# Packed attention and a feed-forward layer on one core: another order of loads, conversions and batch 1's steps in the start of the kernel

## The chip, the cores and the metric

The kernel runs on one core of one Trainium2 chip. The metric is the device time of one execution in microseconds, the median of three runs. Beside the runs there is one profiled execution, from which every row below comes.

## What is computed

For each of 8 batches and 8 heads, 32 packed queries p attend over 576 keys and values; then the 576 queries q attend over the 32 packed results, which serve as keys and as values. The outcome goes through a feed-forward layer with a leaky activation that has its own slope for each of 2048 columns. Inputs are float32 and the output is float32.

```python
def sm_attn(qq, kk, vv):
    s = scale * np.matmul(qq, kk.transpose(0, 1, 3, 2))
    s = s - np.max(s, axis=-1, keepdims=True)
    a = np.exp(s)
    a = a / (np.sum(a, axis=-1, keepdims=True) + 1e-09)
    return np.matmul(a, vv)
p_packed = sm_attn(p, k, v)
out = sm_attn(q, p_packed, p_packed)          # (8, 8, 576, 64)

h = x @ w_in                                  # x: 4608 x 512, w_in: 512 x 2048
g = np.maximum(h, 0.0) + alpha * np.minimum(h, 0.0)
return (g @ w_out).astype(np.float32)         # w_out: 2048 x 512
```

The two weights reach the kernel as 64-bit words (float64) and are made into float32 on the chip.

## The kernel before

**Tiles and stages.** The packed results of a batch are multiplied into w_in first (packed_w, which gives pw), so that the first product of the feed-forward layer takes the softmax of q directly: a step first(k, f) multiplies pw of 128 columns f into the softmax of one half batch k (288 tokens), and ScalarE (L787) and VectorE (L801) make the activation of it; second(k, f) multiplies the activation into piece f of w_out. order lists all pairs (k, f): for k 0 and 1 f 0 to 3, then f 4 to 7, then k 2 and 3 with f 0 to 7, then k 0 to 3 with f 8 to 15, then the other batches in turn. The main loop (i) runs first two steps ahead of second. The first eight steps are plain float32 (L774 and L896); later ones split each number into two parts (L780 to L782, L899 to L901). In the trace a float32 matmul leaves two records.

**Pieces of the weights.** w_in has eight pieces n (two for each group j of 512 columns) and w_out eight pieces g of 256 rows. Each is loaded by one 1 MB transfer (w_in_load, w_out_load) into a raw tile of const; the tags (wo0 to wo7) are shared, so w_in 0, 3 and 4 use one buffer in turn (wo4), w_out 0 and 1 that of batch 0's k, w_out 2 and 3 that of batch 0's v. A piece is converted in one of two ways. to_f32 (a whole piece): the magnitude of the upper words, a conversion of the lower words on ScalarE, then four passes of VectorE (L132, L135, L139, L143). to_half: the magnitude, a sign and a conversion of the lower words on ScalarE (L175, L176), then three passes of VectorE (L166, L169, L177), at half the value. The magnitude is an Abs on ScalarE (L151) or, for w_in 0 alone, a bit mask on VectorE (L123). w_in groups 2 and 3 and all of w_out but piece 2 are halves. Converted w_in goes to DRAM also (w_whole), for the later batches.

**The order.** attention(b) is a generator; each next() traces one part of it up to its yield. For batches 0 and 1 the parts are: 1 loads packed p and k, 2 loads v, 3 loads q, 4 makes the scores of p on k, 5 and 6 the exponentials, 7 and 8 transpose them, 9 multiplies with v, 10 transposes the result (p2), 11 and 12 make the scores of q, 13 to 15 do the softmax of the first half of the tokens (m, the maxima; z, the sums; then the transposition into a_f, L568), 16 to 18 that of the second half. go(what) reads a string: a and b trace the next part of batch 0 and 1, i and o load the next piece of w_in and w_out, I and O convert it, 0 makes a piece of pw for batch 0, H splits a half of batch 0's softmax, S splits one of the first two pieces of w_out, u, v, w and x put spare matmuls on TensorE (keep_busy; v behind m, w behind z). One string stands ahead of the loop, and pieces holds one for some of its steps. turns and joints place the parts of the later batches, PAIRS the pieces of pw for batches 0 and 1.

The instructions of an engine are put into its queue by the tile framework's planner: by the order in which they are traced and by when its costs say that their inputs are there, so a later one may overtake one that is not ready. issue_after forbids that for the pairs it names: in the start string every load is chained to the one traced before it (load, queue), and a conversion stands behind the last ScalarE and VectorE instruction of batch 0 so far (tail). In the loop the pieces stand behind the activation of the step (marks).

Of the kernel before, what the change touches and what calls it, by code (L numbers as in the profile page):

```python
# [27 lines left out]
def pack_attention_ffn_kernel(  # L28
# [90 lines left out]
    def to_f32(raw, mag, on_dve=False):  # L119
        u, up, low = words(raw, "low", U32)  # L120
        bits = mag.bitcast(U32)
        if on_dve:
            nc.vector.tensor_scalar(  # L123
                out=bits, in0=u[:, :, :, 1], scalar1=0x7FFFFFFF, scalar2=None, op0=ALU.bitwise_and
            )
        else:
            magnitude(mag, up)
        with ExitStack() as behind:
            for mark in late + lows:
                behind.enter_context(tc.issue_after(mark.ins))  # L130
            lows[:] = [nc.scalar.activation(out=low, in_=u[:, :, :, 0], func=AF.Copy, scale=2.0**-29)]
        nc.vector.tensor_scalar(  # L132
            out=mag, in0=mag, scalar1=F64_BOTTOM, scalar2=F64_TOP, op0=ALU.max, op1=ALU.min
        )
        nc.vector.tensor_scalar(  # L135
            out=bits, in0=bits, scalar1=3, scalar2=0x3FFFFFF8,
            op0=ALU.logical_shift_left, op1=ALU.bitwise_and,
        )
        nc.vector.scalar_tensor_tensor(  # L139
            out=bits, in0=u[:, :, :, 1], scalar=0xC0000000, in1=bits,  # L140
            op0=ALU.bitwise_and, op1=ALU.bitwise_or,
        )
        last = nc.vector.tensor_tensor(out=bits, in0=bits, in1=low, op=ALU.add)  # L143
        if len(first_half) == 1:
            first_half.append(last)

    def magnitude(mag, up):
# [5 lines left out]
    def to_half(raw, mag, begun=False):  # L153
# [10 lines left out]
        if not begun:  # L164
            magnitude(mag, up)
# [27 lines left out]
    first_half, begun = [], []  # L193
    last_mm, queue, written, raws, tail, whole, w0, other = [], [], [True], {}, {}, [], [], []

    def half(g):
        return g != 2

    def half_in(j):
        return j > 1  # L200
# [5 lines left out]
    def w_out_convert(g):  # L206
# [8 lines left out]
        if half(g):  # L215
            to_half(raws.pop(("o", g)), mag, g in begun)
        else:
            to_f32(raws.pop(("o", g)), mag)
        if g >= QF:
            w_out_split(g, mag)  # L220

    def w_out_begin(g):
        whole.append(const.tile([P, QF, 2, 512], F32, name="wo_whole", tag="wo7"))
        raw = raws["o", g]
        up = raw.bitcast(F32).rearrange("p a (f t) -> p a f t", t=2)[:, :, :, 1]
        nc.scalar.activation(out=whole[0][:, g], in_=up, func=AF.Abs)
        begun.append(g)
# [29 lines left out]
    def w_in_convert(n):  # L257
# [3 lines left out]
        if half_in(j):  # L261
            to_half(raw, w)
        else:
            to_f32(raw, w, n < 1)
# [686 lines left out]
    counts = dict.fromkeys("iIoOSH01A", 0)  # L951
# [3 lines left out]
    def go(what):  # L955


        for ch in what:
# [9 lines left out]
            elif ch in counts:  # L968
# [9 lines left out]
                else:  # L978
                    with ExitStack() as behind:
                        for ins in tail.values() if ch != "A" else []:  # L980
# [3 lines left out]
                            "O": w_out_convert, "S": w_out_late_split, "H": late_a, "A": w_out_begin,  # L984
# [5 lines left out]
    go("inaaauoiaaaIaboaiiaa0abooavbawaOIx")  # L990
# [16 lines left out]
    PAIRS = {13: ((1, 0), (1, 1)), 31: ((0, 2), (1, 2)), 35: ((0, 3), (1, 3))}  # L1007
# [13 lines left out]
    pieces = {0: "aab", 1: "Oai0ib", 3: "bbI", 4: "I", 5: "Oob0", 6: "bbbiO", 7: "HHbb", 10: "S", 11: "S", 12: "b", 13: "bb", 14: "b", 15: "o", 17: "Io", 18: "b", 19: "I", 20: "i", 21: "o", 22: "I", 24: "I", 27: "O", 30: "O", 34: "O", 36: "O"}  # L1021

    X = {1: 50, **{b: begins[b] + 8 for b in range(2, 7)}}
    Y = {1: 54, **{b: begins[b] + 22 for b in range(2, 7)}}
    for b in range(2, B):
        T, x, y = begins[b - 1], X[b - 1], Y[b - 1]
        if b == 2:
            firsts = [39, 40, 41, 42, 44, 45, 46, 47, 49]
        elif b == 3:
            firsts = [44, 50, 61, 62, 63, 64, 66, 67, 68]  # L1030
# [97 lines left out]
```

## Time and profile before

| | |
|---|---|
| median of 3 runs | 711.91 us (711.72 to 712.71) |
| profiled execution | 712.62 us |
| its span | 710.8 us |
| TensorE busy | 695.5 us (98%) |
| VectorE busy | 474.3 us (67%) |
| ScalarE busy | 358.1 us (50%) |
| GpSimd busy | 33.0 us (5%) |
| transfers of SP's queue | 83.89 MB, 36.4% of 16 engines |

The span is the part of the execution from its first to its last recorded instruction. Busy shares are means over a start in which all engines and the transfers are full and a long stretch in which TensorE alone is; what a change in the start is worth has to be read from the start's own rows.

### The profile page before, as it was taken

Reading aid. Unit: us, or ns where it says so; the run is one execution under the profiler, and the core shown is the slowest. Engines: PE = TensorE matmul, PEld = TensorE weight load, DVE = VectorE, ACT = ScalarE, POOL = GpSimd, SP = SyncE. Lnnn points to the kernel's source line nnn. Section 1 sums busy time; section 2 is a strip of 40 time slices with the busy share of each in tenths; the row PEclk is TensorE's granted clock in tenths of the full one; section 3 lists DMA queues with packets and bytes.
Section 4 is the critical chain, followed back from the end, with each engine's and each line's share of the span. In section 5 each row is a group of like instructions: output and inputs, shape, how many; then the busy total and the mean of one; then the engine's idle time right before and its main releaser. Section 6 shows DMA issues by size and latency. Waiting matters only on the chain.

```text
span 710.8 us, 14597 instructions
## 1 busy us (share of the span) xinstructions
PE 695.5 (98%) x5600; PEld 599.2 (84%) x5600; DVE 474.3 (67%) x1067; ACT 358.1 (50%) x846; POOL 33.0 (5%) x128
## 2 busy tenths in 40 slices
PE   6899999999999999999999999999999999999997
PEld 3578998899898888888878888888887888798897
DVE  4999888865796568656773567846694456964443
ACT  3796788944355535444443454545353333533232
POOL 1001200001001200001000010001000000000000
PEclk9899999999999999999999999999999999999999
DMA  9996474133534422452323423334314203010100
GB/s 312 385 342 244 129 261 151 60 104 122 155 117 156 135 59 99 148 156 73 126 47 118 156 68 127 125 100 120 97 59 152 66 7 95 25 30 1 30 16 30
DMA packets 77188, 85.36 MB, mean 120 GB/s; under 512 B 34880, under 2 KB 57920, under 8 KB 77120
## 3 DMA queue, kind: packets, MB, share of 16 engines
q1 hardware_dynamic: 76480, 83.89, 36.4%
q8 instruction: 44, 0.72, 0.4%
q10 hardware_dynamic: 640, 0.56, 0.2%
q14 instruction: 24, 0.20, 0.1%
HBM read 70.79 MB, written 13.63 MB: 119 GB/s over the span
## 4 chain that ended last, share of the span: by engine, by line
PE 92%; DVE 3%; DMA 2%; ACT 2%; issue 0%; SPq 0%; DVEq 0%
PE acc L832 40%; PE ps_h L780 9%; PE ps_h L782 9%; PE ps_h L781 9%; PE acc L899 5%; PE acc L900 5%; PE acc L901 5%; PE ps_m L375 4%; PE ps_j L375 3%; PE acc L896 2%; PE acc L375 2%; DMA wraw<-in_w_out 1%; DMA xtwo<-in_kT 1%; PE ps_h L774 1%; PE spare L286 0%
## 5 line engine op out<-in xcount | busy, mean ns | idle before, releaser
L832 PE MATMUL acc<-wo,gh 128*128 128x512 f32 x704 | 200.1, 398 | 0.0
L787 ACT ACTIVATE neg<-ps_h 128x256 f32<-128x256 f32 (+2 forms) x256 | 105.4, 412 | 164.4 <-PE ps_h L782 157.8
L801 DVE SCALAR_TENSOR_TENSOR neg<-neg,nal,ps_h 128x256 f32<-128x256 f32 (+1 forms) x248 | 119.6, 483 | 77.1 <-ACT neg L787 76.6
L811 ACT CAST gh<-neg 128x256 fp32r<-128x256 f32 (+1 forms) x248 | 101.7, 411 | 111.3 <-DVE neg L801 110.0
L780 PE MATMUL ps_h<-a_h,pw 128*128 128x256 f32 (+2 forms) x496 | 146.4, 295 | 0.8 <-DVE neg L801 0.8
L782 PE MATMUL ps_h<-a_h,pw 128*128 128x256 f32 (+2 forms) x496 | 146.6, 296 | 0.0
L781 PE MATMUL ps_h<-a_l,pw 128*128 128x256 f32 (+2 forms) x496 | 146.5, 295 | 0.0
L812 DVE TENSOR_TENSOR gl<-neg,gh 128x256 fp32r<-128x256 f32 (+1 forms) x248 | 104.4, 425 | 61.5 <-ACT gh L811 59.8
L832 PEld LDWEIGHTS acc<-wo,gh 128*128 128x128 f32 x704 | 126.7, 195 | 21.9 <-issue 4.2
L832 PE MATMUL acc<-wo,gl 128*128 128x512 f32 x352 | 115.5, 394 | 0.0
L780 PEld LDWEIGHTS ps_h<-a_h,pw 128*128 128x128 f32 x496 | 93.5, 188 | 7.6 <-DVE neg L801 1.3
L781 PEld LDWEIGHTS ps_h<-a_l,pw 128*128 128x128 f32 x496 | 93.4, 188 | 7.2
L782 PEld LDWEIGHTS ps_h<-a_h,pw 128*128 128x128 f32 x496 | 93.5, 189 | 0.1
L900 PE MATMUL acc<-gh,wo 128*128 128x288 f32 (+1 forms) x280 | 79.7, 293 | 0.5 <-DVE wo L237 0.5
L832 PEld LDWEIGHTS acc<-wo,gl 128*128 128x128 f32 x352 | 68.7, 195 | 13.5
L899 PE MATMUL acc<-gh,wo 128*128 128x288 f32 (+1 forms) x280 | 80.0, 296 | 0.0
L901 PE MATMUL acc<-gl,wo 128*128 128x288 f32 (+1 forms) x280 | 69.8, 293 | 0.0
L899 PEld LDWEIGHTS acc<-gh,wo 128*128 128x128 f32 x280 | 52.6, 189 | 5.0 <-ACT pw L730 3.4
L900 PEld LDWEIGHTS acc<-gh,wo 128*128 128x128 f32 x280 | 52.8, 189 | 0.7 <-DVE wo L237 0.7
L794 DVE SCALAR_TENSOR_TENSOR rest<-neg,nal,ps_h 128x64 f32<-128x64 f32 x96 | 26.6, 277 | 40.1 <-ACT neg L787 40.1
L901 PEld LDWEIGHTS acc<-gl,wo 128*128 128x128 f32 x280 | 48.6, 188 | 0.7 <-issue 0.5
L832 PE MATMUL acc<-wo,rparts 128*128 128x512 f32 x144 | 35.3, 397 | 0.0
(157 smaller groups left out, 690.1 us busy)
## 6 DMA issues: line engine op xcount, KB each, us to landing
w<-w_whole SPq DMA_DIRECT2D x48, 512.0 KB, 5.8
wraw<-in_w_in SPq DMA_DIRECT2D x8, 1024.0 KB, 10.9
wraw<-in_w_out SPq DMA_DIRECT2D x8, 1024.0 KB, 6.8
xraw<-in_kT SPq DMA_DIRECT2D x28, 288.0 KB, 4.5
xraw<-in_qT SPq DMA_DIRECT2D x28, 288.0 KB, 4.6
vraw<-in_v SPq DMA_DIRECT2D x96, 64.0 KB, 2.1
outT<-out SPq DMA_DIRECT2D x44, 128.0 KB, 2.2
w_whole<-w SPq DMA_DIRECT2D x6, 512.0 KB, 7.6
```

The costliest lines, as they stand in the source:

```text
L375: mm = nc.tensor.matmul(out, lhs, rhs, start=start, stop=stop)
L780: nc.tensor.matmul(x, w[:, 0, i], a_h[:, i], start=(i == 0), stop=False)
L781: nc.tensor.matmul(x, w[:, 0, i], a_l[:, i], start=False, stop=False)
L782: mm = nc.tensor.matmul(x, w[:, 1, i], a_h[:, i], start=False, stop=(i == 1))
L787: marks[:] = [mm, nc.scalar.activation(out=neg, in_=x, func=AF.Relu, scale=-1.0)]
L801: nc.vector.scalar_tensor_tensor(out=g, in0=neg, scalar=nal[:, f : f + 1], in1=x, op0=ALU.mult, op1=ALU.add)
L811: late[:] = [nc.scalar.copy(out=gh, in_=g)]
L812: nc.vector.tensor_tensor(out=gl, in0=g, in1=fv(gh), op=ALU.subtract)
L832: mm = nc.tensor.matmul(ps, g, wo_t[f][:, part_], start=(f == 0 and i == 0), stop=(f == NF - 1 and i == 2))
L899: nc.tensor.matmul(ps, wo_t[f][:, 0, os_], gh, start=begin, stop=False)
L900: nc.tensor.matmul(ps, wo_t[f][:, 1, os_], gh, start=False, stop=False)
L901: mm = nc.tensor.matmul(ps, wo_t[f][:, 0, os_], gl, start=False, stop=end)
```

## The change

Part ahead of the loop: the string is another one. Spelled out, before: w_in 0, alpha, v, q (batch 0), scores, 7 spares, w_out 0, w_in 1, ..., k of batch 1, w_out 1, ..., w_in 2, w_in 3, ..., v of batch 1, w_out 2, w_out 3, ..., q of batch 1. After: alpha, w_in 0, v, w_in 1, q (batch 0), w_out 0, w_out 1, scores, 7 spares, ..., k of batch 1, ..., v of batch 1, ..., w_in 2, w_in 3, w_out 2, w_out 3, w_in 4, ..., q of batch 1. Conversions at its end: w_out 0, w_in 1 before; w_in 1, w_out 0 after. The three spares of x move from the end of the string to a place behind v's; batch 1's scores (part 4) and its first exponential, and parts 16 and 17 of batch 0, move from step 0 into the string.

Conversions: the magnitude of w_in 5 and 6 and of w_out 1, 3, 4 and 5 is a VectorE mask, that of w_in 0 an Abs on ScalarE. Pieces 4 and 5 of w_out are whole, piece 2 is a half. w_out_begin, which no string calls, is gone.

In the loop: pieces, two of the PAIRS, X and Y of batch 1 and the first places of batches 2 and 3 have other steps.

```diff
--- before.py
+++ after.py
@@ -119,12 +119,7 @@
     def to_f32(raw, mag, on_dve=False):
         u, up, low = words(raw, "low", U32)
         bits = mag.bitcast(U32)
-        if on_dve:
-            nc.vector.tensor_scalar(
-                out=bits, in0=u[:, :, :, 1], scalar1=0x7FFFFFFF, scalar2=None, op0=ALU.bitwise_and
-            )
-        else:
-            magnitude(mag, up)
+        magnitude(mag, u, up, on_dve)
         with ExitStack() as behind:
             for mark in late + lows:
                 behind.enter_context(tc.issue_after(mark.ins))
@@ -144,13 +139,18 @@
         if len(first_half) == 1:
             first_half.append(last)
 
-    def magnitude(mag, up):
+    def magnitude(mag, u, up, on_dve):
+        if on_dve:
+            nc.vector.tensor_scalar(
+                out=mag.bitcast(U32), in0=u[:, :, :, 1], scalar1=0x7FFFFFFF, scalar2=None, op0=ALU.bitwise_and
+            )
+            return
         with ExitStack() as behind:
             for ins in lows:
                 behind.enter_context(tc.issue_after(ins.ins))
             nc.scalar.activation(out=mag, in_=up, func=AF.Abs)
 
-    def to_half(raw, mag, begun=False):
+    def to_half(raw, mag, on_dve=False):
 
 
 
@@ -161,8 +161,7 @@
         u, up, rest = words(raw, "rest", F32)
         bits = mag.bitcast(U32)
         low = rest.bitcast(U16).rearrange("p a (f t) -> p a f t", t=2)[:, :, :, 0]
-        if not begun:
-            magnitude(mag, up)
+        magnitude(mag, u, up, on_dve)
         nc.vector.tensor_scalar(
             out=mag, in0=mag, scalar1=F64_BOTTOM_HALF, scalar2=F64_TOP, op0=ALU.max, op1=ALU.min
         )
@@ -190,14 +189,17 @@
         if written:
             queue[:] = [ins]
 
-    first_half, begun = [], []
+    first_half = []
     last_mm, queue, written, raws, tail, whole, w0, other = [], [], [True], {}, {}, [], [], []
 
+    WHOLE_OUT, HALF_IN = (4, 5), (2, 3)
+    ON_DVE_IN, ON_DVE_OUT = (5, 6), (1, 3, 4, 5)
+
     def half(g):
-        return g != 2
+        return g not in WHOLE_OUT
 
     def half_in(j):
-        return j > 1
+        return j in HALF_IN
 
     def w_out_load(g):
         raws["o", g] = const.tile([P, 2, 512], U64, name=f"wraw{g}", tag=f"wo{g}")
@@ -213,18 +215,11 @@
         else:
             mag = cv.tile([P, 2, 512], F32, name="mag", tag="mag")
         if half(g):
-            to_half(raws.pop(("o", g)), mag, g in begun)
+            to_half(raws.pop(("o", g)), mag, g in ON_DVE_OUT)
         else:
-            to_f32(raws.pop(("o", g)), mag)
+            to_f32(raws.pop(("o", g)), mag, g in ON_DVE_OUT)
         if g >= QF:
             w_out_split(g, mag)
-
-    def w_out_begin(g):
-        whole.append(const.tile([P, QF, 2, 512], F32, name="wo_whole", tag="wo7"))
-        raw = raws["o", g]
-        up = raw.bitcast(F32).rearrange("p a (f t) -> p a f t", t=2)[:, :, :, 1]
-        nc.scalar.activation(out=whole[0][:, g], in_=up, func=AF.Abs)
-        begun.append(g)
 
     def w_out_late_split(g):
         w_out_split(g, whole[0][:, g])
@@ -259,9 +254,9 @@
         raw = raws.pop(("i", n))
         w = win.tile([P, 4, 256] if j == 0 else [P, 2, 512], F32, name="w", tag="w")
         if half_in(j):
-            to_half(raw, w)
+            to_half(raw, w, n in ON_DVE_IN)
         else:
-            to_f32(raw, w, n < 1)
+            to_f32(raw, w, n in ON_DVE_IN)
         if j == 0:
             w0.append(w)
             for a in range(2):
@@ -948,7 +943,7 @@
     EARLY, XF, XJ, QF = 2, 1, 1, 2
 
     a0, a1 = attention(0), attention(1)
-    counts = dict.fromkeys("iIoOSH01A", 0)
+    counts = dict.fromkeys("iIoOSH01", 0)
     BUSY = {"u": 7, "v": 4, "w": 2, "x": 3, "y": 3, "z": 2}
     BEHIND = {"v": "m0", "w": "z0", "z": "m1"}
 
@@ -977,17 +972,17 @@
                     packed_w(1, n, (None,) if n else (0, 1))
                 else:
                     with ExitStack() as behind:
-                        for ins in tail.values() if ch != "A" else []:
+                        for ins in tail.values():
                             behind.enter_context(tc.issue_after(ins.ins))
                         {
                             "i": w_in_load, "I": w_in_convert, "o": w_out_load,
-                            "O": w_out_convert, "S": w_out_late_split, "H": late_a, "A": w_out_begin,
+                            "O": w_out_convert, "S": w_out_late_split, "H": late_a,
                         }[ch](n)
 
     go("a")
     with tc.issue_after(other[-1].ins):
         nc.scalar.activation(out=tiny, in_=tiny, func=AF.Copy, bias=2.0**-20)
-    go("inaaauoiaaaIaboaiiaa0abooavbawaOIx")
+    go("niaiaooauabaabIaiaaa0iaoavxaaoiIOabwbab")
     tail.clear()
     written.clear()
 
@@ -1004,7 +999,7 @@
             if b % 2 and k % 2:
                 order += [(b // 2, n, "columns") for n in range(4)]
     turns, joints, drains = {}, {}, []
-    PAIRS = {13: ((1, 0), (1, 1)), 31: ((0, 2), (1, 2)), 35: ((0, 3), (1, 3))}
+    PAIRS = {32: ((0, 3), (1, 3)), 13: ((1, 0), (1, 1)), 29: ((0, 2), (1, 2))}
     for at_, pair in PAIRS.items():
         joints[at_] = [(0, packed_w_pair(*pair))]
 
@@ -1018,16 +1013,16 @@
                 turns.setdefault(at_, []).append(gen)
         drains.append((steps[-1], gen))
 
-    pieces = {0: "aab", 1: "Oai0ib", 3: "bbI", 4: "I", 5: "Oob0", 6: "bbbiO", 7: "HHbb", 10: "S", 11: "S", 12: "b", 13: "bb", 14: "b", 15: "o", 17: "Io", 18: "b", 19: "I", 20: "i", 21: "o", 22: "I", 24: "I", 27: "O", 30: "O", 34: "O", 36: "O"}
-
-    X = {1: 50, **{b: begins[b] + 8 for b in range(2, 7)}}
-    Y = {1: 54, **{b: begins[b] + 22 for b in range(2, 7)}}
+    pieces = {0: 'b0bbb', 1: 'aioH', 3: 'OI', 4: 'IO', 6: 'O0bboi', 9: 'SHb', 10: 'bb', 11: 'S', 13: 'b', 14: 'bi', 16: 'I', 18: 'Ib', 21: 'b', 23: 'I', 25: 'Ioo', 28: 'O', 30: 'O', 33: 'O', 36: 'O'}
+
+    X = {1: 51, **{b: begins[b] + 8 for b in range(2, 7)}}
+    Y = {1: 56, **{b: begins[b] + 22 for b in range(2, 7)}}
     for b in range(2, B):
         T, x, y = begins[b - 1], X[b - 1], Y[b - 1]
         if b == 2:
-            firsts = [39, 40, 41, 42, 44, 45, 46, 47, 49]
+            firsts = [37, 40, 42, 43, 46, 46, 47, 49, 55]
         elif b == 3:
-            firsts = [44, 50, 61, 62, 63, 64, 66, 67, 68]
+            firsts = [48, 50, 61, 62, 64, 64, 65, 66, 67]
         else:
             U = begins[b - 2]
             firsts = [U - 4, *(X[b - 2] + n for n in (0, 2, 3, 4, 5, 6, 7, 8))]
```

## Rows read from the trace of the kernel before

**Rows 1.** The page, part 1: busy us, share of the span, instructions

```profile
PE 695.5 (98%) x5600; PEld 599.2 (84%) x5600; DVE 474.3 (67%) x1067; ACT 358.1 (50%) x846; POOL 33.0 (5%) x128
```

**Rows 2.** TensorE's waits, whole span: us in total, times, longest

```profile
PE ps_m L672 <- DMA vtwo<-in_v: 1.1, 1, 1.1
PE acc L896 <- DVE g L801: 0.7, 1, 0.7
PE ps_h L774 <- ACT pw L724: 0.5, 1, 0.5
PE ps_h L780 <- DVE neg L801: 0.8, 2, 0.4
PE acc L900 <- DVE wo L237: 0.5, 1, 0.5
```

**Rows 3.** Timeline of TensorE: start, us, line, shapes, records, idle before

```profile
16.05 1.49 PE L375 MATMUL acc<-xtwo,p 64*32 64x288 f32 x32 [0.36 <-ACT p L514]
22.03 2.48 PE L286 MATMUL spare<-ident 128*128 128x128 f32 x10
24.30 2.13 PE L774 MATMUL ps_h<-a_f,pw 128*128 128x288 f32 x4
26.36 1.45 PE L375 MATMUL ps_m<-xraw,praw 64*32 64x288 f32 x16
30.85 0.72 PE L375 MATMUL ps_m<-xraw,praw 64*32 64x288 f32 x16
41.57 1.13 PE L774 MATMUL ps_h<-a_f,pw 128*128 128x288 f32 x4
```

**Rows 4.** Two stretches of 1 us: busy by engine, clock, transfers

```profile
20.00:21.00 1.00, 0.15 (x2) 0.00 (x0) 1.00 (x2) 0.53 (x2) 0.00 (x0) 0.95 1.05 375
27.00:28.00 1.00, 1.00 (x17) 0.26 (x2) 1.00 (x3) 0.16 (x1) 0.00 (x0) 0.64 1.02 410
```

**Rows 5.** The same view, longer stretches

```profile
30.00:40.00 10.00, 8.57 (x63) 5.41 (x62) 9.88 (x19) 8.26 (x14) 0.00 (x0) 1.00 0.96 314
80.00:100.00 20.00, 19.63 (x146) 19.18 (x145) 16.86 (x30) 17.27 (x27) 1.80 (x2) 1.00 0.46 158
100.00:150.00 50.00, 49.54 (x454) 45.26 (x453) 40.78 (x73) 39.68 (x71) 0.00 (x0) 1.00 0.41 139
```

**Rows 6.** Two loads: SP's issue, then size and us to landing

```profile
6.38 1.14 SPq L189 DMA_DIRECT2D xtwo<-in_qT  x2
xtwo<-in_qT SPq DMA_DIRECT2D x2, 288.0 KB, 8.2
12.11 0.47 SPq L189 DMA_DIRECT2D wraw<-in_w_in  x1
wraw<-in_w_in SPq DMA_DIRECT2D x1, 1024.0 KB, 11.3
```

**Rows 7.** Timeline of VectorE

```profile
12.41 0.68 DVE L123 TENSOR_SCALAR w<-wraw 128x1024 uint32<-128x1024 uint32 x1
17.09 0.84 DVE L525 STREAM_TRANSPOSE t<-acc 128x288 f32<-128x288 f32 x2
22.35 0.78 DVE L568 STREAM_TRANSPOSE a_f<-t 128x576 f32<-128x576 f32 x1
25.34 0.69 DVE L132 TENSOR_SCALAR w<-w 128x1024 f32<-128x1024 f32 x1 [0.90 <-ACT w L151]
28.11 1.22 DVE L139 SCALAR_TENSOR_TENSOR w<-wraw,w 128x1024 uint32<-128x1024 uint32 x1
```

**Rows 8.** Timeline of ScalarE

```profile
20.70 1.12 ACT L151 ACTIVATE wo_whole<-wraw 128x1024 f32<-128x1024 f32 x1 [0.47 <-DMA wraw<-in_w_out]
24.20 1.11 ACT L151 ACTIVATE w<-wraw 128x1024 f32<-128x1024 f32 x1
```

**Rows 9.** Timeline of GpSimd and VectorE at 88 us

```profile
87.81 1.60 POOL L580 TENSOR_TENSOR a_l<-s,a_h 128x576 fp32r<-128x576 f32 x1 [7.61 <-ACT a_h L579]
88.05 1.92 DVE L166 TENSOR_SCALAR w<-w 128x1024 f32<-128x1024 f32 x1
```

## The prediction

> **What bounds the kernel now.** I read the page's busy times, then TensorE's waits and queue, its clock, the stretches, and last the other queues of the first 60 us, one at a time [rows 1 to 9]. TensorE is busy 695.5 of 710.8 us [rows 1], so the reader should look for the 15.3 us in which it is idle. Most of them lie ahead of the first feed-forward step, which begins at 24.30 [rows 3], and in the stores at the end, which the change does not touch. Between the two there is little left: 0.7 and 0.5 us in the first steps, twice 0.4 us (at 60 and at 93 us) and 0.5 us at 143 us [rows 2], some 2.5 us in all. Idle is not the only loss. The granted clock falls to 0.50 (1.2 of 2.4 GHz) at 20.9 us, after a sparse stretch, and is back at 27.7 [rows 4]. In between the first step's four matmuls take 2.13 where the same four take 1.13 later, and batch 1's first half of scores 1.45 where the second half takes 0.72 [rows 3]: 1.7 us of real work lost. So the change can win at most 2.5 + 1.7 us behind the start, and otherwise only by moving the start.
>
> What sets the start and the pace behind it? VectorE is busy 9.88 of 10 us between 30 and 40, with the transfers at a share of 0.96 [rows 5]. q of batch 0 has its second quarter issued at about 7.1 and landed 8.2 us later, at 15.3; w_in 1 lands at 12.11 + 11.3 = 23.4 [rows 6]; batch 1's k has just landed when its scores run at 26.36 [rows 3]. VectorE comes from the transposition that makes a_f (22.35 + 0.78 = 23.1) and then waits 0.90 us for w_in 1 [rows 7], since ScalarE waited for w_out 0 until 20.70, converted it first and came to w_in 1 at 24.20 [rows 8].
>
> **The change, part by part.**
>
> (1) w_in 1 is put ahead of q of batch 0; the loads of the start string are chained, so this holds. One MB takes 2.7 us here (w_out 0 has landed at 20.70 [rows 8], w_in 1, the next in the queue, at 23.4 [rows 6]). The second quarter of q then lands at 18.0 instead of 15.3. The scores on it stood behind p until 16.05 [rows 3], so 0.7 us of slack is eaten first; they start at 18.0, end their first half (0.72) at 18.7, and VectorE's first transposition of them, which also stood behind the conversion of w_in 0, moves from 17.09 [rows 7] to about 18.7. From there to the end of a_f at 23.1 lies one chain of VectorE and ScalarE work. So a_f comes 1.6 us later, at 24.7. Bounds: 0.8, if two transfers share the engines, to 2.0.
>
> (2) Step 0 began at 24.30 although a_f was there at 23.1: the ten spare matmuls in front ran 2.48 us at the low clock [rows 3]. The change puts six of them ahead of z, so four stay behind it, 1.0 us by the same row, and they end before a_f. First step: 24.7, 0.4 later.
>
> (3) The clock. More filler stands behind m, and the waiting for q makes the stretch from 15.7 to 18.0 emptier. Which wins no row shows. Bounds: the whole 1.7 us back, or the same loss and 0.6 us more. I take 0.6 back, a third. The Trainium skill, TensorE: Matmul & The Clock Gate, Part 1 (The HAM clock gate), says that the throttled state is the default and that activity releases it; by that rule the whole 1.7 us would come back if filler, scores and step 0 join up. The trace agrees in so far as the clock rose at 27.7 only after matmuls had run without a gap from 22.0.
>
> (4) VectorE's pace up to step 8. It is later by 1.6 from (1). The mask of w_in 0 (0.68 [rows 7]) becomes a magnitude on ScalarE, some 1.1 us behind the exponentials of batch 0, beside the 1.1 us in which TensorE waits for v [rows 2]; it saves nothing on VectorE, which then waits for q. Without that cover it would cost 1.1. The 0.90 us wait for w_in 1 goes: it has landed by 17, and its magnitude follows the first exponential. w_out 2 becomes a half piece: of passes of 0.69, 0.69, 1.22 and 1.22 [rows 7] one of 1.22 goes, -1.2. Masks for w_out 1 and w_out 3: +0.7 each, +1.4. One of two splits of batch 0's a, about 0.7 by the passes of like size, goes behind step 8. Sum: 1.6 - 0.9 - 1.2 + 1.4 - 0.7 = +0.2. ScalarE loses two magnitudes of 1.12 [rows 8] and gains one pass of a half piece; it is not the late one any more.
>
> (5) TensorE's pace up to step 8. Its work stays, and without waits and low clock it would gain 0.7 + 0.5 + 1.7 = 2.9, less the 0.4 of (2). VectorE's +0.2 says that it can't: w_out 0 is now converted behind w_in 1, and the second halves of steps 0 and 1 wait for it. The conversion of w_out 1 moves behind step 3, which frees 2.6 us (0.69, 0.69 and 1.22) ahead of the first activations and gives them back two steps later. I take TensorE 0.2 later from VectorE and 0.6 earlier from the clock: -0.4. Bounds -2.5 and +1.6.
>
> (6) Batch 1's scores (1.45 us in two halves of 0.72) are traced ahead of step 0. w_out 1 now stands ahead of their k, so k lands at 26.4 + 2.7 = 29.1. I take it that step 0 overtakes them in TensorE's queue, since nothing chains them to it: 0. The other answer is the second rival.
>
> (7) w_in 4 is loaded in the chained string, ahead of q of batch 1, into the buffer that w_in 3 leaves after its conversion in step 4; SP holds it, and behind it q and every later load. Step 4 lies at 42 to 47 us, and batch 1's scores on q come in step 6 or behind; with some 8 us from issue to landing [rows 6] q is there by 55. I take 0; the cover is a few us, and without it the excess is lost.
>
> (8) Behind step 16: masks for w_in 5, w_in 6, w_out 4 and 5 (+0.7 each), and w_out 4 and 5 whole (+1.2 each): VectorE +5.2 us between 80 and 150, where it is busy 16.9 + 40.8 of 70 us [rows 5]. The last two of TensorE's waits stand here on VectorE [rows 2], and ahead of the one at 93 us VectorE had a pass of 1.92 us, beside GpSimd's 1.60 us [rows 9], where 0.69 is usual [rows 7]. The Trainium skill, GPSIMD Engine Reference, Specifications, speaks against the masks here: GpSimd shares its SBUF interfaces with VectorE and contends with its two-port modes. Batch 1's GpSimd work now spreads over more steps, so a mask may meet it, and a meeting costs VectorE 1.2. I take -0.1 for both waits together; bounds -0.9 and +1.5.
>
> Sum against the profiled execution: 712.62 - 0.4 - 0.1 = 712.1. That execution lies 0.71 above the median of the three runs, so **711.4**.
>
> **The rivals.**
>
> *TensorE's pace holds (faster).* If the clock stays up and VectorE serves the activations first, (5) gives -2.5 and (8) half a us: -3.0, 708.9. For it: VectorE's gap of 0.90 vanishes, and 2.6 us of conversion leave the first steps. Against: VectorE has no other slack before 60 us, and its chain starts 1.6 us later.
>
> *The scores block step 0 (slower).* In TensorE's queue batch 1's scores stand ahead of step 0 and wait for k until 29.1; step 0 begins at about 29.6. By then the kernel before had done two first halves (2.3 at full clock), half the scores (0.7) and 0.7 of a second half, 3.7 in all; the changed one has 1.4 of that behind it: 2.3 later, 714.2, or 713.0 if the conversions done meanwhile spare it the waits of 0.7 and 0.5. It decides from the point where k lands after a_f; if k lands by 24.7, it costs nothing. For it: the order in which the program is written. Against: only the landing times.
>
> *VectorE becomes the bound behind step 16 (same or slower).* 5.2 us more make 82% busy 90%; one mask that meets GpSimd, and one late piece of w_out as at 143 us, give +1.3: 713.2.
>
> *It does not do what its words say.* By the string it is two pieces of w_in, not of w_out, that stand ahead of batch 0's q, and four of w_out stood ahead of step 0 before too. A w_out 0 that comes sooner is then no part of it; it comes 2.7 later. The sum has this already, so it gets no chance of its own.
>
> **How the numbers follow.** Forecast 711.4 with 0.43, its own range 710.2 to 713.0; TensorE's pace 0.25; blocked scores 0.21; VectorE behind step 16 0.11. About 0.2% (1.4 us) is what a measurement of this kernel can tell from no change. Faster: nearly all of the second case and a seventh of the first, 0.31. Slower: four fifths of the third, a third of the last, a few hundredths of the first, 0.24. Same: 0.45. Range 708.7 to 714.2, from just below the one rival to the price of the other.
>
> **What would show it.** (1) q of batch 0 lands after 17.5 and TensorE waits for it. (2) Step 0 begins between 24 and 25.5, with four spares ahead of it. (3) The granted clock from 16 to 30. (4) VectorE waits no longer for w_in 1 and is full to 59. (6) Batch 1's scores ahead of step 0 with a wait on their k is the blocked case. (8) VectorE at about 90% from 80 to 150, with passes over 1.5 us beside GpSimd. I am wrong if q does not land later, or if behind 150 us the time moves by more than 0.3 us.

## The result, and the profile after

The changed kernel takes 715.87 us (median of four runs, 715.04 to 717.02) against 712.04 of the kernel before: ratio 1.0054, 95% interval 1.0036 to 1.0071. It is slower, and outside the predicted range. The profiled execution is the fastest of the four: 715.04 us, span 713.2, 2.4 us over that of before. Line numbers of after lie five lower than those of before in the loop (L769 and L891 are the float32 first and second, L775 and L894 the split ones, L370 the small matmuls, L796 the activation on VectorE, L782 on ScalarE).

Part 1 of after's page (busy us, share, instructions), to be laid beside [rows 1]:

```profile
PE 696.1 (98%) x5600; PEld 596.1 (84%) x5600; DVE 478.7 (67%) x1073; ACT 352.0 (49%) x840; POOL 31.9 (4%) x128
```

TensorE is busy 0.6 us more and idle 1.8 more. Its waits in after (us in total, times, longest), beside [rows 2]:

```profile
PE acc L370 <- DMA xtwo<-in_qT: 2.2, 2, 1.3
PE ps_m L649 <- ACT pw L719: 1.3, 1, 1.3
PE ps_h L769 <- DVE a_f L563: 0.7, 1, 0.7
PE acc L891 <- DVE wo_whole L176: 0.7, 1, 0.7
PE ps_m L370 <- DMA xraw<-in_kT: 0.5, 1, 0.5
```

TensorE now waits for q of batch 0, which it never did before; the 0.7 us on an activation has gone, the 0.5 on the copy of pw has become 1.3, and others have come. TensorE's queue in after (start, us, line, shapes, records, idle before), beside [rows 3]:

```profile
16.34 1.10 PE L370 MATMUL acc<-xtwo,p 64*32 64x288 f32 x12 [1.31 <-DMA xtwo<-in_qT]
19.05 1.46 PE L370 MATMUL acc<-xtwo,p 64*32 64x288 f32 x16 [0.93 <-DMA xtwo<-in_qT]
22.91 0.69 PE L281 MATMUL spare<-ident 128*128 128x128 f32 x4
24.30 1.21 PE L769 MATMUL ps_h<-a_f,pw 128*128 128x288 f32 x4 [0.70 <-DVE a_f L563]
26.01 0.68 PE L370 MATMUL ps_m<-xraw,praw 64*32 64x288 f32 x4 [0.50 <-DMA xraw<-in_kT]
27.79 1.41 PE L370 MATMUL ps_m<-xraw,praw 64*32 64x288 f32 x12
36.21 0.55 PE L649 MATMUL ps_m<-ident,s_t 128*128 128x128 f32 x3 [1.34 <-ACT pw L719]
41.62 1.47 PE L667 MATMUL ps_m<-vraw,aT 128*32 128x64 f32 x80
43.74 4.15 PE L891 MATMUL acc<-g,wo_whole 128*128 128x288 f32 x16 [0.65 <-DVE wo_whole L176]
51.70 1.06 PE L370 MATMUL ps_m<-w,p 64*32 64x512 f32 x8
56.77 1.06 PE L370 MATMUL ps_m<-w,p 64*32 64x512 f32 x8
59.59 0.52 PE L775 MATMUL ps_h<-a_h,pw 128*128 128x288 f32 x1
```

and the rows of before that answer to the last ones:

```profile
50.94 1.09 PE L375 MATMUL ps_m<-w,p 64*32 64x512 f32 x16
55.73 0.51 PE L780 MATMUL ps_h<-a_h,pw 128*128 128x288 f32 x1
56.56 1.50 PE L672 MATMUL ps_m<-vraw,aT 128*32 128x64 f32 x80
```

The first step starts at 24.30 in both kernels, the first split step at 55.73 before and 59.59 after: 3.86 us, of which 1.47 are batch 1's product with v, done at 41.62 instead of 56.56. The 2.4 us that are left are the difference of the spans, so the whole loss of this pair lies between the two steps. This stretch by engine, first in before, then in after (length, then busy us of TensorE, its weight loads, VectorE, ScalarE, GpSimd; then clock, transfer share, GB/s):

```profile
24.30:55.72 31.42, 29.99 (x171) 20.15 (x171) 30.36 (x50) 28.06 (x48) 0.00 (x0) 0.95 1.01 363
```

```profile
30.00:40.00 10.00, 8.64 (x67) 5.59 (x66) 8.09 (x21) 5.79 (x14) 0.00 (x0) 1.00 0.96 340
100.00:150.00 50.00, 49.64 (x454) 45.20 (x453) 44.97 (x77) 36.92 (x67) 0.00 (x0) 1.00 0.39 131
...
24.30:59.58 35.28, 32.63 (x250) 20.99 (x251) 32.78 (x53) 28.00 (x49) 0.57 (x2) 1.00 0.86 295
```

(The rows of 30 to 40 and of 100 to 150 us answer to [rows 5].) The clock stands at 1.00 in this execution of after, without the low clock of [rows 4]. The terms: the product with v +1.47; idle time 2.65 instead of 1.43, +1.2; the fourth piece of pw in two halves of 1.06 each instead of one of 1.09, +1.0; batch 1's first scores 0.68 + 1.41 instead of 1.45 [rows 3], +0.6; the first four matmuls 1.21 instead of 2.13, -0.9. They make +3.4 of 3.9 us; the other half us lies in groups of under 0.3 us that I did not follow.

Two of these terms hang on the clock of the profiled execution of before and not on the change: the 2.13 us of the first four matmuls and the 1.45 of the scores. The run with the changed places behind step 8 alone (below) has before's start string, conversions and first steps, and in its profiled execution the clock stood at 1.00 from 20 to 30:

```profile
23.31 1.21 PE L769 MATMUL ps_h<-a_f,pw 128*128 128x288 f32 x4
24.45 2.45 PE L370 MATMUL ps_m<-xraw,praw 64*32 64x288 f32 x16
55.34 0.51 PE L775 MATMUL ps_h<-a_h,pw 128*128 128x288 f32 x1
```

Beside that execution the changed kernel's first step is 1.0 us late and its first split step 4.25 (2.8 without the product with v). The scores take 2.09 instead of 2.45 there, so that they are no loss. In the pair of profiles above, VectorE has 2.4 us more work between the two steps (32.78 instead of 30.36) and 1.4 us more idle time (2.50 instead of 1.06).

VectorE and ScalarE of after show where the idle time is from; first VectorE:

```profile
17.74 0.85 DVE L520 STREAM_TRANSPOSE t<-acc 128x288 f32<-128x288 f32 x2 [1.60 <-PE acc L370]
23.38 0.78 DVE L563 STREAM_TRANSPOSE a_f<-t 128x576 f32<-128x576 f32 x1
24.08 0.65 DVE L127 TENSOR_SCALAR w<-w 128x1024 f32<-128x1024 f32 x1
38.92 1.00 DVE L796 SCALAR_TENSOR_TENSOR g<-neg,nal,ps_h 128x288 f32<-128x288 f32 x2 [1.77 <-ACT neg L782]
42.46 1.23 DVE L176 CUSTOM_DVE_ANT_0 wo_whole<-wo_whole,rest 128x2048 uint16<-128x2048 uint16 x1 [0.48 <-ACT rest L175]
52.65 1.21 DVE L138 CUSTOM_DVE_ANT_0 w<-w,low 128x2048 uint16<-128x2048 uint16 x1
```

then ScalarE:

```profile
34.27 0.78 ACT L624 ACTIVATE s_t<-s_t,nmx 128x576 f32<-128x576 f32 x1 [0.76 <-DVE nmx L623]
35.04 0.76 ACT L624 ACTIVATE s_t<-s_t,nmx 128x576 f32<-128x576 f32 x1
35.80 0.63 ACT L719 ACTIVATE pw<-ps_m 128x256 f32<-128x256 f32 x2
38.47 0.90 ACT L782 ACTIVATE neg<-ps_h 128x288 f32<-128x288 f32 x2
```

Batch 1's two exponentials (34.27 and 35.04) stand ahead of the copy of pw on ScalarE. TensorE waits 1.34 for that copy, the activation comes 1.77 late to VectorE, the conversion of w_out 1 behind it ends at 42.46 + 1.23 = 43.69, and TensorE waits 0.65 for it. The conversion of w_in 3 ends at 52.65 + 1.21 = 53.86, behind 51.70; so the half of pw whose heads lie in w_in 2 runs ahead, alone.

### The profile page after: what moved, and what is told of

It reads as the page before. It is cut to its first block, busy times and chain, and to the rows that moved or that the text cites. A ratio compares the mean times of both kernels' runs of the same rounds, so it can differ in the third digit from the quotient of the medians.

```text
span 713.2 us, 14597 instructions
## 1 busy us (share of the span) xinstructions
PE 696.1 (98%) x5600; PEld 596.1 (84%) x5600; DVE 478.7 (67%) x1073; ACT 352.0 (49%) x840; POOL 31.9 (4%) x128
## 4 chain that ended last, share of the span: by engine, by line
PE 89%; DVE 6%; DMA 2%; ACT 2%; issue 1%; SPq 0%; DVEq 0%; ACTq 0%
PE acc L827 39%; PE ps_h L775 9%; PE ps_h L777 9%; PE ps_h L776 9%; PE acc L894 4%; PE acc L895 4%; PE acc L896 4%; PE ps_m L370 3%; PE ps_j L370 2%; PE acc L891 2%; PE acc L370 1%; DMA xtwo<-in_qT 1%; DVE pw L726 1%; DVE gl L807 1%; PE ps_h L769 1%
## 5 line engine op out<-in xcount | busy, mean ns | idle before, releaser
L782 ACT ACTIVATE neg<-ps_h 128x256 f32<-128x256 f32 (+2 forms) x256 | 104.9, 412 | 168.7 <-PE ps_h L777 154.0
L796 DVE SCALAR_TENSOR_TENSOR neg<-neg,nal,ps_h 128x256 f32<-128x256 f32 (+1 forms) x248 | 119.6, 483 | 77.3 <-ACT neg L782 76.8
L775 PE MATMUL ps_h<-a_h,pw 128*128 128x256 f32 (+2 forms) x496 | 146.7, 296 | 1.4 <-DVE pw L726 0.7
L775 PEld LDWEIGHTS ps_h<-a_h,pw 128*128 128x128 f32 x496 | 93.5, 188 | 9.2 <-DVE neg L796 1.4
L894 PE MATMUL acc<-gh,wo 128*128 128x288 f32 (+1 forms) x280 | 79.5, 296 | 0.0
L895 PE MATMUL acc<-gh,wo 128*128 128x288 f32 (+1 forms) x280 | 78.5, 293 | 0.0
L896 PE MATMUL acc<-gl,wo 128*128 128x288 f32 (+1 forms) x280 | 67.4, 292 | 0.0
L894 PEld LDWEIGHTS acc<-gh,wo 128*128 128x128 f32 x280 | 52.4, 189 | 5.1 <-ACT pw L725 2.5
```

Of the source, the lines that this page charges most:

```text
L775: nc.tensor.matmul(x, w[:, 0, i], a_h[:, i], start=(i == 0), stop=False)
L782: marks[:] = [mm, nc.scalar.activation(out=neg, in_=x, func=AF.Relu, scale=-1.0)]
L796: nc.vector.scalar_tensor_tensor(out=g, in0=neg, scalar=nal[:, f : f + 1], in1=x, op0=ALU.mult, op1=ALU.add)
L894: nc.tensor.matmul(ps, wo_t[f][:, 0, os_], gh, start=begin, stop=False)
L895: nc.tensor.matmul(ps, wo_t[f][:, 1, os_], gh, start=False, stop=False)
L896: mm = nc.tensor.matmul(ps, wo_t[f][:, 0, os_], gl, start=False, stop=end)
```

## The experiments

Times are medians in us; each ratio is against runs of the kernel before on the same chip. Those runs have medians of 712.0 to 712.7, so that between two tables the ratios are compared, not the times. In the kernel before, batch 1's first exponential stood in step 1; only its scores and parts 16 and 17 of batch 0 stood in step 0.

**One part of the change in the old kernel.** Only the load order:

```diff
-    go("inaaauoiaaaIaboaiiaa0abooavbawaOIx")
+    go("niaiaooauaaaIabaiiaa0abooavbawaOIx")
```

> The kernel before with the order of its loads alone changed: alpha, w_in 0, v, w_in 1, q of batch 0, w_out 0, w_out 1 and then batch 1's k. Rival J (load order): q lands 1.6 us later and batch 1's k 2 us later, step 0 begins at 24.3 or later, and the time is 1 to 2.5 us above before (712.3), to about 714. Theory H: under 0.7 us, since w_in 1 is there sooner and VectorE's 0.9 us wait for it goes.

Only batch 1's parts 5 to 9, moved ahead:

```diff
-    pieces = {0: "aab", 1: "Oai0ib", 3: "bbI", 4: "I", 5: "Oob0", 6: "bbbiO", ...
+    pieces = {0: "aabbb", 1: "Oai0ibbb", 3: "I", 4: "I", 5: "Oo0", 6: "bbiO", ...
```

> The kernel before with parts 5 to 9 of batch 1 moved ahead, to steps 0 and 1, and nothing else. Theory E: the kernel before loses 1 to 2.5 us, to about 713.8, with a gap of TensorE or VectorE of over 1 us between 33 and 45 us that it does not have now. Rivals F and G: within 0.5 us of before (712.1).

Only the conversions (after's code with the string, pieces, PAIRS, X, Y and firsts of before):

> The other half of the change: the conversions of the changed kernel (six masks, w_out 4 and 5 whole, w_out 2 a half) in the order of the kernel before. Theory E: within 0.5 us of before (712.1), since VectorE is not the bound behind step 16 and loses as much as it gains up to step 8. Rival F: slower by 1.5 us or more, with new waits of TensorE on VectorE between 60 and 150 us.

The conversions and all places from step 6 on, with before's string and first steps:

> The kernel before up to step 8, with the changed kernel's conversions and its order behind step 8. Theories H and J (all of the loss comes from the start): the waits that the conversions alone brought between 100 and 150 us (2.1 us) are gone, 712 to 713.3. Rival F (conversions): 714 or more, with TensorE idle for over 1.5 us between 24 and 60 us beyond that of before.

The same places alone, with before's conversions:

```diff
-    WHOLE_OUT, HALF_IN = (4, 5), (2, 3)
-    ON_DVE_IN, ON_DVE_OUT = (5, 6), (1, 3, 4, 5)
+    WHOLE_OUT, HALF_IN = (2,), (2, 3)
+    ON_DVE_IN, ON_DVE_OUT = (0,), ()
```

> The kernel before with the changed kernel's places from step 8 on alone (pieces, PAIRS, X, Y, firsts), the conversions as before. The conversions alone cost +2.1 (714.6), conversions and places together +0.7 (713.6). If the two terms add up, the places alone give -1.4: 711.3. If the places only make room for the longer conversions, they give nothing by themselves: 712.5 to 713.0.

| old kernel with | time | ratio, 95% |
|---|---|---|
| load order | 715.62 | 1.0040, 1.0027 to 1.0053 |
| batch 1's parts 5 to 9 ahead | 715.13 | 1.0036, 1.0023 to 1.0049 |
| conversions | 714.60 | 1.0030, 1.0022 to 1.0039 |
| places behind step 8 | 713.33 | 1.0015, 1.0006 to 1.0024 |
| conversions and places | 713.63 | 1.0010, 1.0002 to 1.0019 |

Each of these parts is slower alone, and the first three and the last but one together would make 1.2%, where the whole change costs 0.5%: the parts don't add up. The rest of the new string, the order of batch 0's steps and of the first conversions, was not tried alone. Conversions and places belong together. The conversions with the old places leave TensorE idle for 2.1 us between 100 and 150; with the new places the idle time of that stretch is as in [rows 5]. The stretch 100 to 150 with the conversions alone, and with both:

```profile
100.00:150.00 50.00, 47.90 (x437) 43.14 (x436) 42.96 (x73) 35.00 (x64) 0.00 (x0) 1.00 0.38 124
```

```profile
100.00:150.00 50.00, 49.64 (x453) 45.19 (x453) 44.32 (x76) 36.53 (x69) 0.00 (x0) 1.00 0.42 135
```

With before's start, conversions and places together cost 0.1%; the rest of the loss lies in the start. Batch 1's parts alone also split the fourth piece of pw in two:

```profile
52.66 1.06 PE L375 MATMUL ps_m<-w,p 64*32 64x512 f32 x8
57.73 1.06 PE L375 MATMUL ps_m<-w,p 64*32 64x512 f32 x8
```

**The two loads apart.** w_in 1 ahead of q of batch 0, and w_out 1 ahead of batch 1's k:

```diff
-    go("inaaauoiaaaIaboaiiaa0abooavbawaOIx")
+    go("niaiaauoaaaIaboaiiaa0abooavbawaOIx")
```

> The kernel before, with one edit in the start string: w_in 1 is loaded ahead of q of batch 0 (alpha, w_in 0, v, w_in 1, q, then w_out 0); w_out 1 stays behind batch 1's k. The two loads together cost this kernel 2.9 us (715.62 against 712.7). Theory 'q carries it': q lands 1.7 to 2.7 us later, a_f 1.6 to 3.0 later, and VectorE, which has no other idle time before step 8, passes it on: 714.0 to 715.6, first split step at 57.5 or later (55.7 in the kernel before). Rival 'k carries it': VectorE makes up for q with conversions that have landed meanwhile, and TensorE finds the scores of batch 1 ready: 712.0 to 713.0.

```diff
-    go("inaaauoiaaaIaboaiiaa0abooavbawaOIx")
+    go("inaaauoiaaaIaobaiiaa0abooavbawaOIx")
```

> The kernel before, with one edit in the start string: w_out 1 is loaded ahead of batch 1's k; q of batch 0 stays where it was. Theory 'q carries it': batch 1's k lands up to 2.7 us later (28 to 29), its scores run behind step 0 and VectorE, which is full then, is not touched: 711.8 to 712.6. Rival 'k carries it': TensorE stands on k for 2 to 3 us in front of work that VectorE needs, and the clock falls again: 713.5 to 715.

714.46 (1.0033, 1.0021 to 1.0045) and 712.92 (1.0007, 0.9999 to 1.0016). In the old kernel q carries the price of the loads. With q late, TensorE's queue:

```profile
17.87 1.83 PE L375 MATMUL acc<-xtwo,p 64*32 64x288 f32 x20 [1.52 <-DMA xtwo<-in_qT]
26.05 1.94 PE L774 MATMUL ps_h<-a_f,pw 128*128 128x288 f32 x4
56.85 0.51 PE L780 MATMUL ps_h<-a_h,pw 128*128 128x288 f32 x1
61.52 0.40 PE L780 MATMUL ps_h<-a_h,pw 128*128 128x288 f32 x1 [0.95 <-DVE neg L801]
```

The first step is 1.75 us later than in [rows 3] and VectorE is busy 9.99 of 10 us between 30 and 40. At the first split step 1.1 of it is left (it stood at 55.73 before), and between 60 and 80 TensorE is idle for 0.95 us, where before it was not: it waits for an activation there. The spans differ by 2.1.

**Undoing a part of the changed kernel.** The conversion of w_out 1 back to step 1; batch 1's parts 5 to 9 back; both; the first exponential traced later; steps 0 to 8 as before; before's conversions:

```diff
-    pieces = {0: 'b0bbb', 1: 'aioH', 3: 'OI', ...
+    pieces = {0: 'b0bbb', 1: 'OaioH', 3: 'I', ...
```

> The changed kernel with the conversion of w_out 1 moved back from step 3 to step 1. Theory A (the lost time is VectorE's idle time: it waits 1.8 us at 37 to 39 us while w_out 1, landed long before, may not be begun, and the second halves of steps 2 and 3 then wait for that piece until 43.7): VectorE has no gap over 0.7 us between 25 and 60 us, the first split step (f = 4) begins at 57.5 to 58.5 instead of 59.6, and the time falls by 1.2 to 2.2 us against the changed kernel (715.9), to about 714.2. Theory B (the later q of batch 0 sets it, a_f comes 1.0 us later than before): under 0.4 us. Theory C (VectorE's additional masks set it): under 0.4 us.

```diff
-    go("niaiaooauabaabIaiaaa0iaoavxaaoiIOabwbab")
+    go("niaiaooauabaabIaiaaa0iaoavxaaoiIOabwba")
-    pieces = {0: 'b0bbb', 1: 'aioH', 3: 'OI', 4: 'IO', 6: 'O0bboi', ...
+    pieces = {0: '0', 1: 'aioHb', 3: 'bbOI', 4: 'IO', 5: 'b', 6: 'O0bbboi', ...
```

> The changed kernel with parts 5 to 9 of batch 1 (exponentials, their transpositions, the product with v) back in the steps in which the kernel before has them: 1, 3, 3, 5 and 6; its scores stay ahead of step 0 and w_out 1 stays in step 3. Theory E (batch 1's softmax, which the first steps do not need, stands in ScalarE's and VectorE's queues ahead of the activations of steps 2 and 3, and TensorE waits behind it): the 1.3 us wait for pw and VectorE's 1.8 us gap go, the third step begins at about 35.2, the first split step at 56.5 to 58 instead of 59.6, and the time falls by 1.5 to 3 us against the changed kernel (715.9), to about 713.7. Rival F (the conversions, masks and whole pieces): under 0.5 us. Rival G (the late w_out 1 together with the later start): VectorE's gap goes but the second halves of steps 2 and 3 still wait for the piece; under 1 us.

```diff
-    pieces = {0: '0', 1: 'aioHb', 3: 'bbOI', ...
+    pieces = {0: '0', 1: 'OaioHb', 3: 'bbI', ...
```

> The changed kernel with two parts taken back together: batch 1's parts 5 to 9 in their old steps, and the conversion of w_out 1 in step 1. Each alone was slower than the changed kernel, one by waiting 2.8 us for w_out 1, the other by exponentials ahead of the activations. Theory H: together they are better than either, 713 to 715. Rival J: 716 or more, as each alone.

> The changed kernel with batch 1's first exponential (part 5) traced behind the second piece of pw instead of ahead of step 0. Theory A2 (ScalarE runs two exponentials of 0.8 us ahead of the copy of pw, and TensorE stands idle for 1.34 us at 35 us): that idle goes, the third step begins at 35.2 to 35.6 instead of 36.6, and the time falls by 0.7 to 1.3 us to about 714.9. If VectorE's idle time behind it is what counts (theory A), under 0.4 us, since its queue then only waits elsewhere. Theories B and C: under 0.3 us.

> The changed kernel with the pieces of steps 0 to 8 as the kernel before has them (conversion of w_out 1 in step 1, batch 1's parts 5 to 9 in steps 1 to 6, the fourth piece of pw in step 5); start string, conversions and everything behind step 8 as changed. Theory H (the order inside steps 0 to 8 is what loses the time; taking back single parts of it only moves the wait): the wait on w_out 1, VectorE's gap and the two separate halves of the fourth piece of pw go together, the first split step begins at 56 to 57.5, and the time is 712 to 713.5. Rival J (the load order and batch 1's scores in the start string): 715 or more.

> The changed kernel's order with the conversions of the kernel before: w_in 0 alone a mask, w_out 2 alone a whole piece. Theory E: the loss stays, within 0.6 us of the changed kernel (715.9). Rival F (the conversions set it): 1.5 us or more less, 714.4 or below.

| changed kernel with | time | ratio to before, 95% |
|---|---|---|
| w_out 1 at step 1 | 717.13 | 1.0067, 1.0054 to 1.0081 |
| batch 1's parts 5 to 9 back | 718.84 | 1.0086, 1.0071 to 1.0101 |
| both | 714.37 | 1.0022, 1.0013 to 1.0031 |
| first exponential later | 715.32 | 1.0047, 1.0031 to 1.0063 |
| steps 0 to 8 as before | 715.44 | 1.0037, 1.0024 to 1.0049 |
| before's conversions | 717.03 | 1.0063, 1.0049 to 1.0076 |

My theory that w_out 1's late conversion alone is the loss fell: putting it back alone did not help (its interval overlaps that of the changed kernel, 1.0036 to 1.0071), and putting batch 1's parts back alone made the kernel slower. With the parts back and w_out 1 still behind step 3, TensorE stands on it:

```profile
43.99 5.53 PE L891 MATMUL acc<-g,wo_whole 128*128 128x288 f32 x16 [2.76 <-DVE wo_whole L176]
```

Both together take the loss from 0.54% to 0.22%, which is 2.1 of the 3.8 us (each against its own runs of the kernel before), with VectorE at 9.99 of 10 us between 30 and 40, the fourth piece of pw in one again, and neither the 1.34 us wait nor that on w_out 1. The two moves have to be judged together. With before's conversions the loss stays, so they don't carry it. With all of steps 0 to 8 as before 0.37% stays: the order inside these steps is not the whole of it either. The exponential traced later changed nothing in the queue; the planner put it ahead of the copy of pw all the same, and the 1.34 us wait stayed.

**q early again in the changed kernel.** q ahead of w_in 1 alone; the same with batch 1's parts and w_out 1 back; with k ahead of w_out 1 too (the diff is against the string with the parts back); and, against that, batch 1's scores traced at step 0:

```diff
-    go("niaiaooauabaabIaiaaa0iaoavxaaoiIOabwbab")
+    go("niaaiooauabaabIaiaaa0iaoavxaaoiIOabwbab")
```

> The changed kernel with q of batch 0 loaded ahead of w_in 1 again. Theory B: q's second quarter lands at 15.4 instead of 17.0, a_f is made at 23.2 instead of 24.2, step 0 begins up to 1 us sooner and the time falls by 0.8 to 1.5 us, to about 714.7. Theory A: step 0 begins sooner, but the first split step by at most 0.4 us, since VectorE's gap and the late w_out 1 stay; under 0.4 us.

> The changed kernel with batch 1's parts 5 to 9 back in steps 1 to 6 and w_out 1 back at step 1 (714.37), and q of batch 0 loaded ahead of w_in 1 again. If q's landing carries what is left, 712.5 to 713.2. If batch 1's k, which still lies behind w_out 1, becomes the next wait, as it did when q alone was moved back in the changed kernel (718.2), 714.5 to 717, with a wait of over 1 us on batch 1's k.

```diff
-    go("niaiaooauabaabIaiaaa0iaoavxaaoiIOabwba")
+    go("niaaioauaboaabIaiaaa0iaoavxaaoiIOabwba")
```

> As the run before it, and w_out 1 is loaded behind batch 1's k too, so that both loads stand as in the kernel before. What is left of the change is then its order of the exponentials and spares in the start string and of conversions 0 and 1, the new masks and whole pieces, and the places behind step 8. If the load order carries what is left of the loss in the start, 712.5 to 713.5 (the kernel before with all edits from step 8 on gave 713.6). If it is the order of the spares, exponentials and conversions in the string, it stays at 714.0 to 715.0.

```diff
-    go("niaaioauaboaabIaiaaa0iaoavxaaoiIOabwba")
+    go("niaaioauaboaabIaiaaa0iaoavxaaoiIOabwa")
-    pieces = {0: '0', ...
+    pieces = {0: 'b0', ...
```

> As the last run (a_b1o1qk: both loads, batch 1's parts 5 to 9 and w_out 1's conversion back, 716.69), and batch 1's scores are traced at step 0 again, which puts them behind step 0's first two matmuls in TensorE's queue; there TensorE stood 3.7 us on batch 1's k at 23.6, ahead of the spares of z and of step 0, and step 0 began at 27.37. If scores that stand ahead of step 0 are what undoes the earlier q, step 0 begins before 24.5 and the time falls by 2.5 to 3.5 us, to 713.2 to 714.2. Rival: VectorE, which had 6.77 of 10 us between 20 and 30 there, is late for another reason (the order of the conversions, w_in 1 ahead of w_out 0), and the time stays within 1 us of 716.7.

In this order: 718.23 (1.0066, 1.0045 to 1.0086), 717.67 (1.0077, 1.0062 to 1.0092), 716.69 (1.0061, 1.0049 to 1.0073), 714.64 (1.0030, 1.0020 to 1.0041). Earlier q made the first no faster and the second slower (1.0022 with q late): TensorE ran into batch 1's k, 1.77 and 1.57 us. TensorE's queue in the third:

```profile
23.57 1.17 PE L370 MATMUL ps_m<-xraw,praw 64*32 64x288 f32 x4 [3.71 <-DMA xraw<-in_kT]
27.37 2.29 PE L769 MATMUL ps_h<-a_f,pw 128*128 128x288 f32 x4
```

and in the fourth:

```profile
22.44 1.21 PE L769 MATMUL ps_h<-a_f,pw 128*128 128x288 f32 x4 [0.70 <-ACT low L126]
23.80 2.84 PE L370 MATMUL ps_m<-xraw,praw 64*32 64x288 f32 x16
```

The third and the fourth differ only in where batch 1's scores are traced, and by 0.31%: 2.05 us as the times stand, 2.6 against the kernel before on each chip, where 2.5 to 3.5 had been expected. That is the prediction's second rival, shown in this variant: the scores stand ahead of step 0 in TensorE's queue and hold it until k comes. In the changed kernel, and with q alone early, they stand between the first two steps, where TensorE waits 0.50 and 1.77 us for k. In the fourth variant the first step begins 1.9 us sooner than in [rows 3] and the first split step 1.1 us later (56.82). 0.3% over before stays, more than conversions and places explain, although q and k land as before; the fourth piece of pw is in two groups there (1.31 and 1.06 us), w_in 1 is still loaded and converted ahead of w_out 0, and w_in 2 and 3 lie behind batch 1's v. Which of these holds the rest wasn't tried.

**The filler.** The old kernel with x's three spares behind v:

```diff
-    go("inaaauoiaaaIaboaiiaa0abooavbawaOIx")
+    go("inaaauoiaaaIaboaiiaa0abooavxbawaOI")
```

> The kernel before with the last three spares moved from the end of the start string to behind the four that follow m. Theory D (the place of the filler keeps the clock at 2.4 GHz, as in the changed kernel, where it never falls): granted clock 1.00 from 20 to 28 us instead of 0.50, the first step's four matmuls take 1.2 instead of 2.1 us, and the time falls by 1.0 to 1.8 us against before (712.0), to about 710.6. Rival (the clock was kept by the other order of the real work, q's wait or batch 1's scores): the clock falls again and the time stays within 0.4 us.

712.08 (0.9996, 0.9988 to 1.0005).

```profile
54.70 0.51 PE L780 MATMUL ps_h<-a_h,pw 128*128 128x288 f32 x1
59.36 0.40 PE L780 MATMUL ps_h<-a_h,pw 128*128 128x288 f32 x1 [0.96 <-DVE neg L801]
```

The first step began at 23.32, 1.0 earlier than in [rows 3], and the first split step was 1.0 earlier too. Then TensorE waited 0.96 us for an activation of VectorE, where it had waited 0.4 before [rows 2], and the time is the same. The clock, which the run was to hold, still fell: it stood at 0.83 on average from 20 to 30 us.

## Why the prediction was wrong

**Step 1** had the right mechanism. q's first two quarters land at 16.2 and 17.0 instead of 14.6 and 15.3, the other two at 19.0 and 19.8 instead of 16.1 and 16.8; a_f is there at 24.16 instead of 23.13: +1.0 where +1.6 was taken and 0.8 to 2.0 allowed. That it came inside the bounds is luck in part: v landed 1.1 us sooner here (12.9 instead of 14.0), which the step did not have and no run explains. With w_in 1 ahead of q in the old kernel, where v landed at 14.4, the second quarter came at 18.5 and the first step 1.75 us late.

**Step 2** is right: 24.30, with four spares ahead (24.7 forecast).

**Step 3** is the first to fail. It counted 0.6 us of the low clock as won time, and the low clock was worth nothing in the old kernel: of 21 of its executions in one comparison the eight with a mean clock of 0.999 or 1.0 have spans of 709.9 to 711.7, the eight at 0.997 or less 709.9 to 711.9. At the first split step the execution at 1.00 shown above is 0.4 us ahead of the profiled one (55.34 and 55.73), and nothing of it is left in the spans. The run with the moved spares says the same: its first steps were 1.0 earlier, and its time the same. In that run a matmul that starts earlier only waits longer for VectorE. Nor is it shown that the change holds the clock up: it stood at 1.00 in the profile, but the four executions of the changed kernel have mean clocks of 0.995 to 1.0, and in both kernels it differs from one execution to the next.

**Step 5** is the second, and the larger one. "Its work stays" is wrong: the fourth piece of pw fell in two groups, +1.0 us of TensorE. And "gives them back two steps later" priced the conversion of w_out 1 behind step 3 at nothing; behind ScalarE's exponentials it cost 0.65 on top of 1.34. Batch 1's parts 5 to 9 and the conversion of w_out 1, undone together, give 2.1 of the 3.8 us back. Step 4 counted VectorE's passes (+0.2) but not its waits: it stood 1.77 us on ScalarE, and from 30 to 40 it was busy 8.09 us, not 9.9. I had followed the moved exponentials on VectorE and on TensorE and left out the queue that they stand in, ScalarE's. Step 4 also let the later q cost 0.7 (1.6 less the 0.9 of the wait that goes); alone in the old kernel it cost 1.1 at the first split step and 2.1 in the span.

What holds the other 1.7 us stays open. Conversions and places have 0.1% of it; the loads cost 0.4% in the old kernel, but q put early again won nothing in the changed one.

**Step 6**: step 0 did overtake the scores, as forecast. k lands in four parts (from 25.9 to 28.5, where 29.1 was forecast), and the scores ran as they landed, in two groups of 2.09 us together. The 0.72 of [rows 3] is for a k that is all there, so the split is no cost of the change: in the old kernel at full clock they took 2.45.

**Step 7** holds: no wait on w_in 4 or on q of batch 1.

**Step 8** holds in the kernel as changed: TensorE is busy 49.64 of 50 us between 100 and 150, VectorE at 44.97. The third rival, VectorE as the bound there, appears only with the conversions at the old places (47.90). With before's start, conversions and places together cost 0.1%, inside the bounds of this step but on the other side of the -0.1 us taken.

The pair of profiles shows 2.4 of the 3.8 us. The other executions of the changed kernel have spans of 713.9, 714.2 and 715.2, the longest at the lowest clock (0.995); with q early but batch 1's parts ahead it is plainer (712.4 at 0.999, 714.0 to 716.7 at 0.990 to 0.994). It seems that these kernels pay for a low clock where the old one does not, perhaps since TensorE now does its start's work late; that is read from the spans alone and not shown, since the profile of the changed kernel is of an execution at 1.0.

## What to carry to other kernels

Where one engine is full, price a reordering by the start of that engine's chain and by every queue that its inputs stand in; a us won on the engine with the largest busy share need not be a us of the kernel's time. Compare stretches at the same clock before a difference is put down to the change. When work is traced earlier, ask of each group of small matmuls whether all its inputs still arrive together. Moves that were made together should be undone together before one of them is called harmful.

## What the runs showed of the hardware

Eight tiles of 64x32 run side by side: sixteen records of 64x512 take 1.09 us, and eight of them, the heads of one piece of w_in, take 1.06. A group that is split in two therefore costs twice. The Trainium skill, TensorEngine Tiling (Array Packing), Key Properties, says that different tiles can load weights and multiply in parallel; the trace agrees, and shows what is lost when the program's order keeps half of them back.

A 1 MB load put ahead of q in the same queue delays q by about its own length. w_in 1 landed 2.6 us behind the last part of v, with q next, in the changed kernel (12.9, 15.5) and in the old one with that one edit (14.4, 17.0); 2.7 had been taken.

SP's queue has at most eight transfers under way: in both traces each further one is issued only when the eighth before it has landed. So in after the first part of batch 1's k is issued at 15.48, when w_in 1 has landed (6.06 + 9.4), while before it went at 14.03, when the last part of v had. A load put ahead of others thus also moves the issue of those behind it. Whether the chip or the program's semaphores set the eight was not tried.

```profile
6.06 0.59 SPq L188 DMA_DIRECT2D wraw<-in_w_in  x1
wraw<-in_w_in SPq DMA_DIRECT2D x1, 1024.0 KB, 9.4
15.48 3.87 SPq L188 DMA_DIRECT2D xraw<-in_kT  x4
```
